# Taking both parts of x through one 512-column product in eight of twelve chunks, with VectorE adding the two sums

## The chip, the cores and the metric

The program runs on one core of a Trainium2 chip. Its engines, as the profile names them: PE (TensorE, matmul) with PEld (its weight loads), DVE (VectorE), ACT (ScalarE), POOL (GpSimd) and SP (SyncE, which issues the DMAs). The metric is the device time of one execution in microseconds; before the change three runs gave 743.53 (median), 743.38 and 745.63.

## The reference

Sliding-window attention with sink columns, followed by one two-layer block over all tokens:

```python
scores = scale * q @ k.T             # 4 batches, 8 heads, 768 positions, head_dim 64
keep = (pos_k < n_sink) | ((rel >= 0) & (rel < window))   # 4 and 128
a = softmax(where(keep, scores, -1e9))
x = (a @ v), heads side by side      # 3072 tokens x 512
h = x @ w_in                         # 512 -> 2048
sp = where(h > 20, h, log1p(exp(min(h, 20))))
out = (h * tanh(sp)) @ w_out         # 2048 -> 512
```

The weights are float64 and the rest is float32.

## The kernel before

The 3072 tokens are worked in 12 chunks of 256 tokens (T = 256, two row blocks of 128). For a chunk, four pairs of heads go through attention (`pair`): scores on PE (L386, L389), masking and row minimum on DVE (L397), exponential on ACT (L400), normalising (L404 to L411), transposes on PE (L421, L430), and the product with v (L439, L443) into a PSUM tile `att`. Its result is the chunk's x, transposed: for each pair of heads, 128 features by 256 tokens.

The matmuls run on float32r operands. To keep float32's precision, a value is split into an upper part, rounded to float32r, and a lower part, the rest; a product is then upper times upper, upper times lower and lower times upper. So x is stored as xh (a copy, L447) and xl (a subtraction on DVE, L448); a weight is prepared once as `wih`/`wil` or `woh`/`wol` in the first third of the span.

The two layers go in 8 steps per chunk (`step`), each over 256 of the 2048 hidden features, that is two blocks y of 128. The first layer fills one PSUM tile `hp` of 128 x 2 x 256, one half for each y. For a block there are four slices kt of 128 features of x and three products of 256 columns for each slice (L477, L478): weight upper by xh, weight upper by xl, weight lower by xh. A step therefore has 24 products of 256 columns, and all three sums land on the same 256 columns. There are two `hp` buffers. Then the activation runs on the whole 128 x 512 tile: Exp from PSUM (L486), a minimum on DVE (L487), Square, Ln and Exp on ACT (L488 to L490), and on DVE the product with `hp` (L491), which writes `n`. The second layer needs `gh`, a rounded copy of n (mostly ACT, L248), and `gl`, the difference (L261 on DVE or L259 on POOL, by the planner's choice). It adds 8 products of 512 columns with gh and 4 with gl to two accumulators `acc` (L506).

The order of all work is set before the program is built: `Plan.solve` takes tasks with a priority, a cost for each engine that may do them, and buffers, and always places next the task that can start earliest; `emit` then writes each engine's instructions in that order. A task is a group of instructions, such as six products of the first layer. A cost marked `shared` is not placed beside POOL work. Where the planner leaves PE without work for 250 ns or more, `emit` fills in products with zeros (L601). The first three chunks are interleaved, while weights are still being prepared; the other nine follow one by one, each chunk's attention running ahead during the chunk before it. The last chunk has no attention beside it.

Of the kernel before, what the change touches and what calls it, by code (L numbers as in the profile page):

```python
# [23 lines left out]
P = 128  # L24
# [33 lines left out]
def f32(ap):  # L58
    return ap.bitcast(F32)
# [6 lines left out]
def dve_t(n, fast=False):  # L66
    return ((n / 2 if fast else n) + 66) / 0.96
# [11 lines left out]
def pe_t(*ns):  # L79
    return sum(n / 2.4 + 13.3 for n in ns)  # L80
# [24 lines left out]
class Plan:  # L105
# [6 lines left out]
    def add(self, prio, ways, deps=(), bufs=(), new=()):  # L112
        deps = {id(d): d for d in list(deps) + [b.maker for b in bufs] if d is not None}
        t = Task(prio, ways, list(deps.values()), list(bufs) + list(new), list(new))
        for b in t.bufs:
            b.users += 1
        for b in new:
            b.maker = t
        self.tasks.append(t)
        return t  # L120
# [104 lines left out]
class Fast(Base):  # L225
# [128 lines left out]
    def pair(self, b, c3, pr, rank, x, x_done):  # L354
# [81 lines left out]
        def out():  # L436
# [4 lines left out]
            if not first:  # L441
# [1 line left out]
                    yield nc.tensor.matmul(o.t[:, i * P:(i + 1) * P], vr.t[:, i, :], sks.t, start=False, stop=i == TB - 1)  # L443
        cost = sum(c1 - c0 for _, c0, c1, _, _ in jobs) / .6 + 200 + (0 if first else T / .6 + 50)
        a = add(r + .05, {PE: (cost, out)}, last + ldv + vdeps, [pth, vt] + ([] if first else [vr, sks]), [o])
        (h, l), k, newx = x[pr // 2], pr % 2, pr % 2 == 0
        a = add(r + .15, self.copy_ways(T, lambda: h.t[:, k, :], lambda: o.t, True), [a], [o] + ([] if newx else [h]), [h] if newx else [])  # L447
        c = add(r + .17, self.sub_ways(T, lambda: l.t[:, k, :], lambda: o.t, lambda: f32(h.t[:, k, :]), (DVE,)), [a],  # L448
                [o, h] + ([] if newx else [l]), [l] if newx else [])
        x_done += [a, c]  # L450

    def jobs(self, first):
# [3 lines left out]

    def step(self, st, f2, rank, begins, ends, wdeps, last):

        nc, add = self.nc, self.plan.add
        if begins:
            st.acc, st.tail = [Buf("acc", [P, DM]) for _ in range(TB)], None
        x, acc = st.x, st.acc
        (wih, woh), (wil, wol) = ((w["wi"], w["wo"]) for w in (self.wh, self.wl))
        r = rank - (SH if last else 0)
        hp = Buf("att" if last and f2 % 2 else "hp", [P, 2, T])
        eager = last and f2 >= NF // 2 - QUICK
        g1 = []
        for y in range(2):  # L470
            f = 2 * f2 + y
            for kh in range(2):
                def first(f=f, y=y, kh=kh):
                    for kt in (2 * kh, 2 * kh + 1):
                        fs = slice(kt * P, (kt + 1) * P)
                        xh, xl = x[kh]
                        for n_, (w_, x_) in enumerate(((wih[f], xh), (wih[f], xl), (wil[f], xh))):  # L477
                            yield nc.tensor.matmul(hp.t[:, y, :], w_.t[:, fs], x_.t[:, kt % 2, :], start=kt == 0 and n_ == 0,  # L478
                                                   stop=kt == KT - 1 and n_ == 2)
                fr = y == 0 and kh == 0  # L480
                g1.append(add(r + .1 + .1 * y + .05 * kh, {PE: (pe_t(*[T] * 6), first)},
                              st.x_done[4 * kh:4 * kh + 4] + wdeps[f][0:2] + g1[-1:], list(x[kh]) + ([] if fr else [hp]), [hp] if fr else []))
        u, m = Buf("u", [P, 2, T]), Buf("n", [P, 2, T])
        gh, gl = Buf("gh", [P, 2, T], F32R), Buf("gl", [P, 2, T], F32R)
        N = 2 * T
        a = add(r + .5, {ACT: (act_t(N, True), lambda: nc.scalar.activation(u.t, hp.t, AF.Exp))}, g1, [hp], [u])  # L486
        a = add(r + .51, {DVE: shared((dve_t(N, True), lambda: nc.vector.tensor_scalar(u.t, u.t, E20, None, ALU.min)))}, [a], [u])  # L487
        a = add(r + .52, {ACT: (act_t(N, ptr=1), lambda: nc.scalar.activation(u.t, u.t, AF.Square, bias=self.one))}, [a], [u])  # L488
        a = add(r + .53, {ACT: (act_t(N, ptr=1), lambda: nc.scalar.activation(u.t, u.t, AF.Ln, bias=self.half, scale=0.5))}, [a], [u])  # L489
        a = add(r + .54, {ACT: (act_t(N), lambda: nc.scalar.activation(u.t, u.t, AF.Exp, scale=-1.0))}, [a], [u])  # L490
        e = add(r + .55, {DVE: (dve_t(N), lambda: nc.vector.scalar_tensor_tensor(m.t, u.t, 1.0, hp.t, ALU.subtract, ALU.mult))}, [a], [u, hp], [m])  # L491
        gg = add(r + .57, self.copy_ways(N, lambda: gh.t, lambda: m.t), [e], [m], [gh])
        gk = add(r + .58, self.sub_ways(N, lambda: gl.t, lambda: m.t, lambda: f32(gh.t)), [gg], [m, gh], [gl])
        if eager:
            del gk.ways[POOL]
            del gg.ways[ACT]
        r = rank
        for y, t, part in self.order(last and f2 == NF // 2 - 1):
            f = 2 * f2 + y
            new = begins and y == 0 and not part  # L500
            done = ends and y == 1 and part == 1

            def second(f=f, y=y, t=t, part=part, new=new, done=done):
                ts_ = slice(t * P, (t + 1) * P)
                for n_, (g_, w_) in enumerate(((gl, woh[f]),) if part else ((gh, woh[f]), (gh, wol[f]))):
                    yield nc.tensor.matmul(acc[t].t, g_.t[:, y, ts_], w_.t, start=new and n_ == 0, stop=done)  # L506
            st.tail = add(r + 1.45 + .2 * part + (.05 * y + .1 * t if last else .1 * y + .05 * t), {PE: (pe_t(*[512] * (2 - part)), second)},
                          [gk if part else gg, st.tail] + wdeps[f][2:4], [gl if part else gh] + ([] if new else [acc[t]]), [acc[t]] if new else [])
            if done:
                self.store(st, r, t, f2 == NF // 2 - 1)  # L510
# [34 lines left out]
    def run(self):  # L545
        self.plan = Plan(self.TAGS)
        self.setup()
        chunks = sorted(((b, c3) for b in range(B) for c3 in range(NCH)), key=lambda z: (z[1] > 0, z))
        self.wh, self.wl = ({"wi": [], "wo": []} for _ in range(2))
        wdeps = [self.weights(f, f * WA + WB) for f in range(NF)]  # L550
        states = []
        for n, (b, c3) in enumerate(chunks):
            st = SimpleNamespace(row=b * S + c3 * T, x_done=[], part={})
            st.x = [(Buf("w", [P, 2, T], F32R), Buf("w", [P, 2, T], F32R)) for _ in range(2)]
            for pr in range(NPAIR):
                self.pair(b, c3, pr, self.att_rank(n, pr), st.x, st.x_done)
            states.append(st)
        seq = self.sequence(len(chunks))
        for r, (n, f2) in enumerate(seq):
            begins, ends = r == 0 or seq[r - 1][0] != n, r + 1 == len(seq) or seq[r + 1][0] != n  # L560
            self.step(states[n], f2, r, begins, ends, wdeps, n == len(chunks) - 1)
        self.emit(self.plan.solve())

    def att_rank(self, n, pr):
# [307 lines left out]
```

## Time and profile before

| | before |
|---|---|
| median of three runs, us | 743.53 |
| profiled execution, us | 743.74 |
| its span, first to last instruction, us | 741.4 |
| PE busy, us (share of the span) | 728.5 (98%) |
| ACT busy, us | 585.4 (79%) |
| DVE busy, us | 474.0 (64%) |
| POOL busy, us | 136.4 (18%) |

The span is what one execution takes between its first and last instruction; some 2.3 us lie around it in the execution's own time. Matmuls are pipelined: a PE row's duration runs from the start to the modelled end of one product, and the next starts long before that. What a product takes from the stream is read from one start to the next.

### The profile page before, as it was taken

The page shows a single profiled execution, that of the slowest core. Times are in us where ns is not written, and L with a number is a line of the kernel's source. Part 1 is how long each engine was busy: PE and PEld are TensorE (multiplying, and loading weights), DVE is VectorE, ACT ScalarE, POOL GpSimd, SP SyncE. Part 2 cuts the span into 40 slices and gives each one's busy share as a digit, 9 for nine tenths or more (in the row PEclk, how much of TensorE's full clock was granted, in tenths as well). Part 3 has the DMA queues.
Part 4 walks back from the last instruction along what each step waited for, and adds up shares of the span by engine and source line. Part 5 has one row for each costly group of instructions (what it writes and reads, how often), then busy time and mean ns, then how long its engine had stood idle before and what let it go on. Part 6 is the DMA issues. An engine that isn't in the chain of part 4 may idle for free.

```text
span 741.4 us, 13855 instructions
## 1 busy us (share of the span) xinstructions
PE 728.5 (98%) x5042; PEld 638.5 (86%) x5042; DVE 474.0 (64%) x1258; ACT 585.4 (79%) x1284; POOL 136.4 (18%) x96
## 2 busy tenths in 40 slices
PE   8999999999999999999999999999999999999996
PEld 5767888888888888988898989889988999899995
DVE  6899899998676655557665556465555555543322
ACT  5999998887778778787778888887888788875753
POOL 0454431232001102200001211121122121110000
PEclk9999999999999999999999999999999999999999
DMA  6654333432342422422332333224313331100000
GB/s 190 180 161 131 121 130 114 137 114 57 107 131 60 103 73 79 106 73 72 92 94 72 90 77 91 72 59 99 100 43 79 105 75 43 49 18 1 29 1 34
DMA packets 48989, 64.17 MB, mean 87 GB/s; under 512 B 4880, under 2 KB 41744, under 8 KB 48912
## 3 DMA queue, kind: packets, MB, share of 16 engines
q1 hardware_dynamic: 48912, 63.20, 30.5%
q8 instruction: 42, 0.69, 0.4%
q14 instruction: 35, 0.29, 0.1%
HBM read 56.89 MB, written 6.29 MB: 85 GB/s over the span
## 4 chain that ended last, share of the span: by engine, by line
PE 82%; ACT 12%; DVE 3%; DMA 1%; issue 0%; ACTq 0%
PE acc L506 32%; PE hp L478 30%; PE att L439 5%; PE att L389 5%; PE att L421 4%; PE att L443 3%; ACT p L400 2%; ACT p L411 2%; PE att L478 2%; ACT w L280 2%; ACT w L248 1%; DMA raw<-w_out 1%; ACT pth L248 1%; ACT u L490 1%; ACT raw L290 1%; ACT u L489 1%
## 5 line engine op out<-in xcount | busy, mean ns | idle before, releaser
L478 PE MATMUL hp<-w,w 128*128 128x256 f32 x2208 | 299.7, 286 | 0.9 <-DVE n L491 0.8
L478 PEld LDWEIGHTS hp<-w,w 128*128 128x128 f32 x2208 | 277.6, 190 | 7.5 <-DVE n L491 1.9
L506 PE MATMUL acc<-w,gh 128*128 128x512 f32 x768 | 197.2, 394 | 0.0
L506 PEld LDWEIGHTS acc<-w,gh 128*128 128x128 f32 x768 | 136.8, 189 | 23.6 <-issue 0.5
L491 DVE SCALAR_TENSOR_TENSOR n<-u,hp 128x512 f32<-128x512 f32 x92 | 62.9, 685 | 72.8 <-ACT u L490 45.3
L506 PE MATMUL acc<-w,gl 128*128 128x512 f32 x384 | 107.6, 395 | 0.0
L400 ACT ACTIVATE p<-p,nm 128x288 f32<-128x288 f32 (+1 forms) x192 | 95.3, 497 | 12.4 <-DVE nm L397 12.3
L488 ACT ACTIVATE u<-u,bias 128x512 f32<-128x512 f32 x96 | 69.1, 721 | 35.5 <-DVE u L487 35.5
L487 DVE TENSOR_SCALAR u<-u 128x512 f32<-128x512 f32 x96 | 44.2, 461 | 74.7 <-ACT u L486 74.5
L397 DVE CUSTOM_DVE_ANT_0 p<-att,m 128x288 f32<-128x288 f32 (+1 forms) x192 | 75.7, 418 | 16.4 <-PE att L389 13.0
L506 PEld LDWEIGHTS acc<-w,gl 128*128 128x128 f32 x384 | 70.8, 188 | 14.4 <-DVE gl L261 0.3
L248 ACT ACTIVATE gh<-n 128x512 fp32r<-128x512 f32 x93 | 58.2, 626 | 27.9 <-DVE n L491 27.6
L411 ACT ACTIVATE p<-p,rc 128x288 f32<-128x288 f32 (+2 forms) x129 | 61.2, 502 | 23.0 <-DVE rc L405 22.5
L259 POOL TENSOR_TENSOR raw<-raw,raw 64x896 fp32r<-64x896 f32 x21 | 44.5, 2121 | 169.3 <-ACT raw L248 107.0
L486 ACT ACTIVATE u<-hp 128x512 f32<-128x512 f32 x92 | 54.3, 590 | 25.2 <-PE hp L478 24.7
L489 ACT ACTIVATE u<-u,bias 128x512 f32<-128x512 f32 x96 | 69.0, 720 | 2.1
L261 DVE TENSOR_TENSOR gl<-n,gh 128x512 fp32r<-128x512 f32 x74 | 52.5, 710 | 26.5 <-ACT gh L248 13.5
L490 ACT ACTIVATE u<-u 128x512 f32<-128x512 f32 x96 | 60.0, 626 | 1.7
L421 PE MATMUL att<-ident,p 128*128 128x128 f32 x352 | 55.6, 275 | 2.9 <-DVE rc L404 1.3
L259 POOL TENSOR_TENSOR gl<-n,gh 128x512 fp32r<-128x512 f32 x22 | 29.2, 1329 | 152.7 <-ACT gh L248 114.8
L439 PE MATMUL att<-pth,vt 128*64 128x128 f32 (+1 forms) x504 | 47.9, 322 | 0.4 <-ACT pth L248 0.2
L421 PEld LDWEIGHTS att<-ident,p 128*128 128x128 f32 x352 | 40.9, 140 | 8.4 <-ACT p L411 1.9
(83 smaller groups left out, 817.0 us busy)
## 6 DMA issues: line engine op xcount, KB each, us to landing
raw<-k_p SPq DMA_DIRECT2D x64, 224.0 KB, 3.6
raw<-w_in SPq DMA_DIRECT2D x16, 512.0 KB, 3.7
raw<-w_out SPq DMA_DIRECT2D x16, 512.0 KB, 4.1
w<-q_p SPq DMA_DIRECT2D x64, 128.0 KB, 3.5
y<-u SPq DMA_DIRECT2D x24, 256.0 KB, 2.2
vt<-v_b SPq DMA_DIRECT2D x32, 192.0 KB, 2.5
vsr<-v_s SPq DMA_DIRECT2D x32, 128.0 KB, 2.3
ks<-k_p SPq DMA_DIRECT2D x15, 144.0 KB, 2.2
```

The costliest lines, as they stand in the source:

```text
L248: ways[ACT] = act_t(n, psum), lambda: nc.scalar.activation(dst(), src(), AF.Copy, scale=scale or 1.0)
L259: ways[POOL] = pool_t(n), lambda: nc.gpsimd.tensor_tensor(dst(), a(), b(), ALU.subtract)
L397: a = add(r + .03 + .01 * e, {DVE: (dve_t(n) + 8, lambda st=st, pv=pv, nm=nm, e=e, mask=mask, n=n: nc.vector.tensor_tensor_reduce(out=pv() ...
L400: a = add(r + .05 + .01 * e, {ACT: (act_t(n, ptr=2), lambda pv=pv, nm=nm, sm=sm, e=e: nc.scalar.activation(pv(), pv(), AF.Exp, bias=nm.t[: ...
L411: ACT: (act_t(n, ptr=1), lambda row=row, rc=rc, e=e: nc.scalar.activation(row(), row(), AF.Copy, scale=rc.t[:, e:e + 1]), 0, PEN_N),
L421: yield nc.tensor.transpose(pt.t[:, e, x * P:(x + 1) * P], p2.t[:, i, e, cols[x]:cols[x] + P], self.ident)
L439: yield nc.tensor.matmul(o.t[e * D:(e + 1) * D, o0:o1], vt.t[:, e, j, :], pth.t[:, e, c0:c1], start=n_ == 0, stop=first and n_ == len(jobs ...
L478: yield nc.tensor.matmul(hp.t[:, y, :], w_.t[:, fs], x_.t[:, kt % 2, :], start=kt == 0 and n_ == 0, stop=kt == KT - 1 and n_ == 2)
L488: a = add(r + .52, {ACT: (act_t(N, ptr=1), lambda: nc.scalar.activation(u.t, u.t, AF.Square, bias=self.one))}, [a], [u])
L489: a = add(r + .53, {ACT: (act_t(N, ptr=1), lambda: nc.scalar.activation(u.t, u.t, AF.Ln, bias=self.half, scale=0.5))}, [a], [u])
L490: a = add(r + .54, {ACT: (act_t(N), lambda: nc.scalar.activation(u.t, u.t, AF.Exp, scale=-1.0))}, [a], [u])
L506: yield nc.tensor.matmul(acc[t].t, g_.t[:, y, ts_], w_.t, start=new and n_ == 0, stop=done)
```

## The change

In chunks 3 to 10 (`wide`), xh and xl of a slice lie side by side in one tile of 128 x 2 x 256. One product of 512 columns takes both with the weight's upper part, and writes two separate sums: upper by xh in the first half of the PSUM tile, upper by xl in the second. The product of the weight's lower part with xh, 256 columns as before, is added to the first half. A tile `hp` now holds one block y, so a step uses two of them; a `tensor_reduce` on DVE adds the two halves into `n`, one instruction for each y, as soon as that block is done. The activation and the last multiplication then read `n` in SBUF in place of `hp` in PSUM, and the multiplication (now `shared` for the planner) writes over `n`. The other four chunks compute as before, with x kept in the new layout.

```diff
-        (h, l), k, newx = x[pr // 2], pr % 2, pr % 2 == 0
-        a = add(r + .15, self.copy_ways(T, lambda: h.t[:, k, :], lambda: o.t, True), ...)
-        c = add(r + .17, self.sub_ways(T, lambda: l.t[:, k, :], lambda: o.t, lambda: f32(h.t[:, k, :]), (DVE,)), [a], ...)
+        h = x[pr]
+        a = add(r + .15, self.copy_ways(T, lambda: h.t[:, 0, :], lambda: o.t, True), [a], [o], [h])
+        c = add(r + .17, self.sub_ways(T, lambda: h.t[:, 1, :], lambda: o.t, lambda: f32(h.t[:, 0, :]), (DVE,)), [a], [o, h])
...
-        hp = Buf("att" if last and f2 % 2 else "hp", [P, 2, T])
+        if not wide:
+            hp = Buf("att" if last and f2 % 2 else "hp", [P, 2, T])
         for y in range(2):
             f = 2 * f2 + y
+            if wide:
+                hp = Buf("hp", [P, 2, T])
             for kh in range(2):
...
+                        if wide:
+                            yield nc.tensor.matmul(hp.t, wih[f].t[:, fs], xt, start=kt == 0, stop=False)
+                            yield nc.tensor.matmul(hp.t[:, 0, :], wil[f].t[:, fs], xt[:, 0, :], start=False, stop=kt == KT - 1)
+                            continue
...
+            if wide:
+                hs.append(add(r + .3 + .1 * y, {DVE: (dve_t(2 * T), lambda y=y, hp=hp: nc.vector.tensor_reduce(
+                    m.t[:, y, :], hp.t.rearrange("p z t -> p t z"), mybir.AxisListType.X, ALU.add))}, ...))
+        h = m if wide else hp
-        a = add(r + .5, {ACT: (act_t(N, True), lambda: nc.scalar.activation(u.t, hp.t, AF.Exp))}, g1, [hp], [u])
+        a = add(r + .5, {ACT: (act_t(N, not wide), lambda: nc.scalar.activation(u.t, h.t, AF.Exp))}, hs or g1, [h], [u])
...
-        e = add(r + .55, {DVE: (dve_t(N), lambda: nc.vector.scalar_tensor_tensor(m.t, u.t, 1.0, hp.t, ALU.subtract, ALU.mult))}, [a], [u, hp], [m])
+        way = dve_t(N), lambda: nc.vector.scalar_tensor_tensor(m.t, u.t, 1.0, h.t, ALU.subtract, ALU.mult)
+        e = add(r + .55, {DVE: shared(way) if wide else way}, [a], [u, h], [] if wide else [m])
...
-            st.x = [(Buf("w", [P, 2, T], F32R), Buf("w", [P, 2, T], F32R)) for _ in range(2)]
+            st.x = [Buf("w", [P, 2, T], F32R) for _ in range(KT)]
```

What this does to the order is shown at three places. First PE, in the middle of the kernel before: one block y of the first layer, after the scores of a pair (the `w` on the left of the comma is a part of x, the other a part of a weight).

```order
L389 MATMUL att_2176_1_5021<-raw_2032_0_4702,w_1963_0_4540 128x288
L478 MATMUL hp_2177_0_5026<-w_1659_0_3830,w_898_0_2137 128x256
L478 MATMUL hp_2177_0_5026<-w_1662_0_3836,w_898_0_2137 128x256
L478 MATMUL hp_2177_0_5026<-w_1659_0_3830,w_903_0_2143 128x256
L478 MATMUL hp_2177_0_5026<-w_1659_0_3830,w_898_0_2137 128x256
L478 MATMUL hp_2177_0_5026<-w_1662_0_3836,w_898_0_2137 128x256
L478 MATMUL hp_2177_0_5026<-w_1659_0_3830,w_903_0_2143 128x256
```

The same place of a wide chunk in the changed kernel, a whole block y, up to the next one:

```order
L443 MATMUL att_1748_0_3930<-sks_1730_0_3900,vsr_1616_0_3660 128x128 x2
L483 MATMUL hp_1755_0_3948<-w_1359_0_3127,w_563_0_1436 128x512
L484 MATMUL hp_1755_0_3948<-w_1359_0_3127,w_573_0_1453 128x256
L483 MATMUL hp_1755_0_3948<-w_1441_0_3297,w_563_0_1436 128x512
L484 MATMUL hp_1755_0_3948<-w_1441_0_3297,w_573_0_1453 128x256
L483 MATMUL hp_1755_0_3948<-w_1522_0_3466,w_563_0_1436 128x512
L484 MATMUL hp_1755_0_3948<-w_1522_0_3466,w_573_0_1453 128x256
L483 MATMUL hp_1755_0_3948<-w_1615_0_3658,w_563_0_1436 128x512
L484 MATMUL hp_1755_0_3948<-w_1615_0_3658,w_573_0_1453 128x256
L421 MATMUL att_1765_0_3971<-ident_100,p2_1712_0_3860 128x128 x4
L483 MATMUL hp_1768_0_3978<-w_1359_0_3127,w_621_0_1553 128x512
```

Three products of a slice have become two, and each block y has an `hp` tile of its own.

Second DVE, in the kernel before, from one step's minimum (L487) to that step's multiplication (L491) and beyond:

```order
L487 TENSOR_SCALAR u_2193_0_5075<-u_2193_0_5075 128x512
L251 COPY pth_2206_0_5101<-att_2184_0_5049 128x2x256
L261 TENSOR_TENSOR w_2123_0_4910<-att_2197_0_5082,w_2120_0_4904 128x256
L491 SCALAR_TENSOR_TENSOR n_2218_0_5118<-u_2193_0_5075,hp_2177_0_5026 128x512
L397 ISA p2_2223_0_5137,nm_2223_1_5138<-att_2220_0_5122,m2_114 128x288
L397 ISA nm_2223_1_5138 128x1
L261 TENSOR_TENSOR gl_2224_0_5141<-n_2218_0_5118,gh_2221_0_5128 128x512
```

DVE in a wide chunk of the changed kernel, from one step's multiplication (now L501, with `n` on both sides) to the next step's minimum (now L497):

```order
L501 SCALAR_TENSOR_TENSOR n_1774_0_3993<-u_1780_0_4004,n_1774_0_3993 128x512
L493 TENSOR_REDUCE n_1802_0_4048<-hp_1792_0_4024 128x256
L404 TENSOR_SCALAR rc_1805_0_4057<-sm_1793_2_4031 128x2
L405 RECIPROCAL rc_1805_0_4057<-rc_1805_0_4057 128x2
L261 TENSOR_TENSOR gl_1809_0_4063<-n_1774_0_3993,gh_1804_0_4055 128x512
L410 TENSOR_SCALAR p2_1793_0_4029<-p2_1793_0_4029,rc_1805_0_4057 128x288
L493 TENSOR_REDUCE n_1802_0_4048<-hp_1803_0_4050 128x256
L497 TENSOR_SCALAR u_1818_0_4080<-u_1818_0_4080 128x512
```

The two reductions (L493) stand between the steps, the second directly ahead of the minimum whose input it feeds through ACT's Exp.

Third PE at the first wide step of the changed kernel. The order of PE's products before this place is the same in both kernels up to some 150 products ahead of it.

```order
L389 MATMUL att_1288_1_2973<-raw_1139_0_2651,w_1214_0_2812 128x288
L421 MATMUL att_1292_0_2983<-ident_100,p2_1222_0_2834 128x128 x4
L612 LDWEIGHTS zero_75
L612 MATMUL acc_1260_0_2920<-zero_75 128x224
L612 LDWEIGHTS zero_75
L612 MATMUL acc_1260_0_2920<-zero_75 128x224
L517 MATMUL acc_1255_0_2906<-w_1070_0_2501,gh_1291_0_2981 128x512
```

Here two products with zeros are filled in that the kernel before does not have. They are the only ones that were added, and none follows them; there are 164 in the kernel before and 166 now. Over the whole program 1024 products of 256 columns (2208 to 1184) became 512 of 512 columns. On DVE 128 reductions are new; the planner also moved work: the subtraction of the keys' parts (64 x 896) goes 30 times to DVE (11 before) and 2 times to POOL (21), the gl subtraction 59 times to DVE (74) and 37 to POOL (22), and the copy of x's upper part out of PSUM 15 times to DVE (38) and 33 to ACT (10).

## Rows read from the trace of the kernel before

**Rows 1.** The page: span, busy shares, PE and its clock in 40 slices.

```profile
span 741.4 us, 13855 instructions
PE 728.5 (98%) x5042; PEld 638.5 (86%) x5042; DVE 474.0 (64%) x1258; ACT 585.4 (79%) x1284; POOL 136.4 (18%) x96
PE   8999999999999999999999999999999999999996
PEclk9999999999999999999999999999999999999999
```

**Rows 2.** Busy time by stage (windows of 50 us), from 200 to 650 us.

```profile
core 0: us, PE busy (x) PEld busy (x) DVE busy (x) ACT busy (x) POOL busy (x), PEclk, DMA share, GB/s
200.00:250.00 50.00, 50.00 (x345) 44.25 (x345) 31.14 (x84) 39.16 (x87) 4.69 (x3) 1.00 0.36 99
...
600.00:650.00 50.00, 50.00 (x359) 44.96 (x358) 28.46 (x76) 41.31 (x90) 10.27 (x6) 1.00 0.20 56
sum 450.00, PE 450.00 PEld 403.01 DVE 266.12 ACT 362.14 POOL 75.75; mean PE 50.00 PEld 44.78 DVE 29.57 ACT 40.24 POOL 8.42
```

**Rows 3.** Chain that ended last, in order of time: start, length (us), what.

```profile
193.19 2.95 PE acc L506 x12
...
347.35 2.87 PE hp L478 x24
...
538.67 2.75 PE acc L506 x12
```

**Rows 4.** Two steps in the middle, all engines: start, length (us), engine, line, operation.

```profile
468.27 0.61 ACT L248 ACTIVATE gh<-n 128x512 fp32r<-128x512 f32 x1
...
472.06 1.70 PEld L506 LDWEIGHTS acc<-w,gh 128*128 128x128 f32 x8
...
472.38 0.60 ACT L486 ACTIVATE u<-hp 128x512 f32<-128x512 f32 x1
...
476.37 0.63 ACT L248 ACTIVATE gh<-n 128x512 fp32r<-128x512 f32 x1 [0.76 <-DVE n L491]
...
478.74 1.69 PEld L506 LDWEIGHTS acc<-w,gh 128*128 128x128 f32 x8
...
480.69 1.07 PE L506 MATMUL acc<-w,gl 128*128 128x512 f32 x4
...
481.60 0.56 PE L389 MATMUL att<-raw,w 128*128 128x288 f32 x3
```

**Rows 5.** PE alone over a step and the start of the next two.

```profile
404.28 2.00 PE L506 MATMUL acc<-w,gh 128*128 128x512 f32 x8
...
412.53 2.00 PE L506 MATMUL acc<-w,gh 128*128 128x512 f32 x8
...
419.20 1.09 PE L506 MATMUL acc<-w,gh 128*128 128x512 f32 x4
```

**Rows 6.** Groups by line: instructions near the reduction, the activation and the moved work.

```profile
L491 DVE SCALAR_TENSOR_TENSOR n<-u,hp 128x512 f32<-128x512 f32 x92 | 62.9, 685 | 72.8 <-ACT u L490 45.3 <-PE att L389 24.3 <-PE hp L478 2.2
L261 DVE TENSOR_TENSOR gl<-n,gh 128x512 fp32r<-128x512 f32 x74 | 52.5, 710 | 26.5 <-ACT gh L248 13.5 <-PE acc L506 12.7
L251 DVE COPY pth<-att 128x512 f32<-128x512 f32 (+1 forms) x28 | 18.5, 661 | 10.2 <-PE att L421 9.4
L251 DVE CAST w<-att 128x256 fp32r<-128x256 f32 x38 | 16.1, 423 | 6.3 <-PE att L443 5.1 <-PE att L439 0.5
L261 DVE TENSOR_TENSOR raw<-raw,raw 64x896 fp32r<-64x896 f32 x11 | 12.0, 1089 | 1.2 <-ACT raw L248 0.9
L486 ACT ACTIVATE u<-hp 128x512 f32<-128x512 f32 x92 | 54.3, 590 | 25.2 <-PE hp L478 24.7
L490 ACT ACTIVATE u<-u 128x512 f32<-128x512 f32 x96 | 60.0, 626 | 1.7
L259 POOL TENSOR_TENSOR gl<-n,gh 128x512 fp32r<-128x512 f32 x22 | 29.2, 1329 | 152.7 <-ACT gh L248 114.8 <-PE hp L478 18.9 <-PE att L421 13.3
L601 PE MATMUL acc<-zero 128*128 128x224 bf16 x164 | 21.0, 272 | 0.0
```

More of the change, by code (lines that the diff above doesn't have):

```diff
@@ L445, in pair @@
         a = add(r + .05, {PE: (cost, out)}, last + ldv + vdeps, [pth, vt] + ([] if first else [vr, sks]), [o])
-        (h, l), k, newx = x[pr // 2], pr % 2, pr % 2 == 0
-        a = add(r + .15, self.copy_ways(T, lambda: h.t[:, k, :], lambda: o.t, True), [a], [o] + ([] if newx else [h]), [h] if newx else [])
-        c = add(r + .17, self.sub_ways(T, lambda: l.t[:, k, :], lambda: o.t, lambda: f32(h.t[:, k, :]), (DVE,)), [a],
-                [o, h] + ([] if newx else [l]), [l] if newx else [])
+        h = x[pr]
+        a = add(r + .15, self.copy_ways(T, lambda: h.t[:, 0, :], lambda: o.t, True), [a], [o], [h])
+        c = add(r + .17, self.sub_ways(T, lambda: h.t[:, 1, :], lambda: o.t, lambda: f32(h.t[:, 0, :]), (DVE,)), [a], [o, h])
         x_done += [a, c]
@@ L455, in jobs, with step @@
         return (1, P, 2 * T - P, 0, T), (0, 0, P, 0, P), (2, 2 * T - P, 2 * T, P, T)
-    def step(self, st, f2, rank, begins, ends, wdeps, last):
+    def step(self, st, f2, rank, begins, ends, wdeps, last, wide):
         nc, add = self.nc, self.plan.add
@@ L466, in step @@
         r = rank - (SH if last else 0)
-        hp = Buf("att" if last and f2 % 2 else "hp", [P, 2, T])
         eager = last and f2 >= NF // 2 - QUICK
[L469 to L482, printed above, removed]
         u, m = Buf("u", [P, 2, T]), Buf("n", [P, 2, T])
@@ L485, in step, with first @@
         N = 2 * T
-        a = add(r + .5, {ACT: (act_t(N, True), lambda: nc.scalar.activation(u.t, hp.t, AF.Exp))}, g1, [hp], [u])
+        g1, hs = [], []
+        if not wide:
+            hp = Buf("att" if last and f2 % 2 else "hp", [P, 2, T])
+        for y in range(2):
+            f = 2 * f2 + y
+            if wide:
+                hp = Buf("hp", [P, 2, T])
+            for kh in range(2):
+                def first(f=f, y=y, kh=kh, hp=hp):
+                    for kt in (2 * kh, 2 * kh + 1):
+                        fs, xt = slice(kt * P, (kt + 1) * P), x[kt].t
+                        if wide:
+                            yield nc.tensor.matmul(hp.t, wih[f].t[:, fs], xt, start=kt == 0, stop=False)
+                            yield nc.tensor.matmul(hp.t[:, 0, :], wil[f].t[:, fs], xt[:, 0, :], start=False, stop=kt == KT - 1)
+                            continue
+                        for n_, (w_, z) in enumerate(((wih[f], 0), (wih[f], 1), (wil[f], 0))):
+                            yield nc.tensor.matmul(hp.t[:, y, :], w_.t[:, fs], xt[:, z, :], start=kt == 0 and n_ == 0,
+                                                   stop=kt == KT - 1 and n_ == 2)
+                fr = kh == 0 and (wide or y == 0)
+                g1.append(add(r + .1 + .1 * y + .05 * kh, {PE: (pe_t(*([2 * T, T] * 2 if wide else [T] * 6)), first)},
+                              st.x_done[4 * kh:4 * kh + 4] + wdeps[f][0:2] + g1[-1:], x[2 * kh:2 * kh + 2] + ([] if fr else [hp]), [hp] if fr else []))
+            if wide:
+                hs.append(add(r + .3 + .1 * y, {DVE: (dve_t(2 * T), lambda y=y, hp=hp: nc.vector.tensor_reduce(
+                    m.t[:, y, :], hp.t.rearrange("p z t -> p t z"), mybir.AxisListType.X, ALU.add))}, [g1[-1]], [hp, m] if y else [hp], [] if y else [m]))
+        h = m if wide else hp
+        a = add(r + .5, {ACT: (act_t(N, not wide), lambda: nc.scalar.activation(u.t, h.t, AF.Exp))}, hs or g1, [h], [u])
         a = add(r + .51, {DVE: shared((dve_t(N, True), lambda: nc.vector.tensor_scalar(u.t, u.t, E20, None, ALU.min)))}, [a], [u])
@@ L560, in run @@
             begins, ends = r == 0 or seq[r - 1][0] != n, r + 1 == len(seq) or seq[r + 1][0] != n
-            self.step(states[n], f2, r, begins, ends, wdeps, n == len(chunks) - 1)
+            self.step(states[n], f2, r, begins, ends, wdeps, n == len(chunks) - 1, GROUP <= n < len(chunks) - 1)
         self.emit(self.plan.solve())
```

## The prediction

> **What bounds the kernel now.** I read the page first. PE is busy 98% of the span, at the full clock in all 40 slices but for the two ends [rows 1]. A busy share alone could still hide waits, so the second view is the stages: from 200 to 650 us PE is busy 450.00 of 450 us, while ACT has 362 and DVE 266, that is 80% and 59% [rows 2]. The reader is to see that in this stretch no other engine is ever waited for, and that only what PE streams can be won there. The third view is the chain, for the price of that stream: it strings together runs of like products from start to start. 24 products of 256 columns take 2.87 us, 119.6 ns each; 12 of 512 columns take 2.75 us, 229.2 ns each [rows 3]. Twice the columns cost less than twice the time: a product has a part that does not grow with its columns. The fourth view, all engines in two steps, says how far the work behind PE is from being late [rows 4].
>
> **The sum on PE.** Per slice kt the change replaces two products of 256 columns by one of 512, and leaves the third. 8 chunks x 8 steps x 2 blocks x 4 slices are 512 replacements. Two products of 256 take 239.2 ns. For one of 512 the rows give three prices. The chain's ordinary run has 229.2 ns: 10.0 ns saved, 5.1 us in all. The four gl products from 480.69 to the next task at 481.60 have 227.5 ns [rows 4]: 11.7 ns saved, 6.0 us. The worst run of the chain has 2.95 us for 12, 245.8 ns [rows 3]: 6.6 ns lost, +3.4 us in all. The first two are nearly all of the stream and lie close together; the worst stands at 193 us, at the end of the crowded early stage, and I keep it for the range. I take the middle of the first two, 5.6 us. Weight loads fall by 512 as well, but PEld is busy 403 of 450 us beside a full PE [rows 2] and ends nothing, so I cost them at nothing; that the fixed part of a product may be a piece of its load is already in the measured prices.
>
> Against this stand two filled-in products of zeros at the first wide step, the only new ones. All 164 before took 21.0 us [rows 6], 0.128 us each: 0.3 us. They also say that the planner sees one pause there and no other of its filling size later.
>
> **What is added on DVE.** 128 reductions, each reading 128 x 512 from PSUM and writing 128 x 256. No row shows a reduction. From below: if it cost by what it writes, the 128 x 256 copy out of PSUM has 423 ns. By what it reads: the 128 x 512 copy out of PSUM has 661 ns, the multiplication with a PSUM operand 685. From above, two passes: 1370 ns, twice the latter [rows 6]. I take 685: it reads 512 elements and has an operand in PSUM, as that row does. Two steps last from 404.28 to 419.20, so one has 7.46 us [rows 5], of which DVE is busy 59%, 4.40 us. Two reductions make it 5.77 of some 7.37 us, 78%. The multiplication with both inputs in SBUF goes from 685 to the 710 ns of the gl subtraction, ACT's Exp from 590 to the 626 of L490 [rows 6]. The planner's moves about cancel on DVE: 19 more key subtractions of 1089 ns add 20.7 us, 15 fewer gl subtractions of 710 ns and 23 fewer copies of 423 ns take 20.4 us away. So neither DVE nor ACT comes to bound a step by its load; PE's 100% is the cover under which all of this costs nothing.
>
> **What it does to the latency.** The added reduction is a wait: Exp of a step now starts only after the second reduction, and PE's second layer waits for gh. What stands before it in DVE's order is listed with the change: the previous gl subtraction and a normalisation. In the rows of before, gh is ready at 468.27 + 0.61 = 468.88 and its first weight load starts at 472.06, 3.18 us later; in the next step gh is ready at 477.00 and loaded at 478.74, 1.74 us later [rows 4]. The steps alternate, the shorter one being that without the product with v. The chain grows by the second reduction 0.685, the Exp 0.036 and the multiplication 0.025, 0.75 us, and the time given to it shrinks by 8 x 10.9 ns, 0.09. So about 0.9 us are left in the tight steps, 2.3 in the others. The `hp` buffers cannot be what is late next: a buffer was held through Exp, four more operations and the multiplication, and is now free after its reduction, so two for a step last longer than two for two steps did. The two `n` buffers are held longer instead, from the first reduction to the gl subtraction, about the time that an `hp` was held before.
>
> **Total.** 743.74 (the profiled execution, 0.2 us over the median of the runs) - 5.6 + 0.3 = 738.4 us. The first 150 us, the last chunk and the output are unchanged by the order.
>
> **Rivals.**
> *Queueing gives it back.* The tight steps have 0.9 us left. A key subtraction of 1089 ns that DVE has begun when the second reduction could start, or a gl subtraction of 0.71 and a normalisation of 0.38 before it as in the listed order, is 0.15 to 0.2 us more than that. In all 32 tight steps this makes 4.8 to 6.4 us, and the time 743.2 to 744.8. For it: DVE's order is fixed and it is 78% full. Against it: PE may stand at other work then, since the order was made with the reductions in it and shows no filling product, and at 80% load ACT kept every such wait from PE. The multiplication may be held up as well: POOL is busy 75.75 of 450 us [rows 2], mostly in reads of SBUF, and a gl subtraction there takes 1329 ns [rows 6]; meeting one half-way in 17% of the steps would be 0.11 us a step on average, inside the 0.9. The Trainium skill bears on this point (SBUF — State Buffer, Who interferes with whom): a VectorE instruction with two SBUF inputs contends with a GpSimd one that reads SBUF, where one with a PSUM operand does not. By that rule the change makes L491's successor open to such waits, by the trace they fit in the slack; it moves this rival's chance from 0.08 to 0.10.
>
> *Only columns count.* In the alternation of 512 and 256 columns the fixed part could stay, because each product has a new weight to load and the stream has as many columns as before. Then nothing is won, and the time is 743.74 + 0.3 = 744.0. Rows 3 speak against it: both sorts of product there had a load each, and 229.2 is less than 239.2. The Trainium skill has a rule near this (TensorE: Matmul & The Clock Gate, Back-to-back issue gap): warm products follow each other by N/2.4 ns and a fixed 2.5 ns. By that rule the 512 merged products would save 1.3 us and the time would be 742.7; the trace disagrees, with 119.6 ns for 256 columns where the rule has 109. Chance 0.05.
>
> *The reduction is dear.* At 1370 ns, two of them take 2.74 us a step, DVE is at 4.40 + 2.74 + 0.03 of 7.37 us, 97%, and the slack of a tight step falls to 1.74 - 1.37 - 0.06 - 0.09 = 0.22 us. Any instruction ahead of it, some 0.7 us, then makes PE wait about 0.5 us; in 32 steps 16 us, and the time is about 754. It decides from a reduction of about 1.0 us on, where one such instruction ahead eats what is left. For it: it reads its input at a stride of 256 elements, two at a time, which no row shows. Against it: nothing in the rows has a 512-element DVE operation on float32 beyond 0.7 us save those that convert. The Trainium skill calls this operation the slowest of VectorE and advises against it on a hot path (VectorE: DVE Perf Modes, Rules for kernel authors); no run here shows it yet. Chance 0.09.
>
> **How the numbers follow.** Forecast 0.76, queueing 0.10, only columns 0.05, dear reduction 0.09. What this kernel's measurement can tell from no change is about 0.3%, 2.2 us. The forecast's own range is 737 to 741 (the two prices of the product, and a microsecond or two of small waits). Queueing and only columns end within 0.3% and are 0.15, of which I give 0.02 to slower, for queueing that goes on past its price; 0.02 of the forecast falls within 0.3% by its upper tail. So faster 0.74, same 0.15, slower 0.11. The range of 8 in 10 goes from 736 to 744, up to the two rivals in the middle, and leaves out the dear reduction and the worst price of a product.
>
> **What would show it.** In the profile after: PE still busy all of each 50 us window in the wide chunks; a slice's two products some 347 ns apart from the next slice's (227.5 to 229.2 + 119.6); `n<-hp` TENSOR_REDUCE x128 near 0.68 us; DVE near 78% in those windows; no waits of PEld for gh or for an `hp` buffer. Wrong would be: a reduction above 1 us, PE waiting for `n` or gh in every second step, or 512-column products at 235 ns and more.

## The result and the profile after

The changed kernel takes 740.0 us (median of 7 runs, 738.4 to 741.59); the kernel before, on the same chips, 744.35 us (7 runs, 743.38 to 745.63). The ratio is 0.9947, with a 95% interval of 0.9935 to 0.9959: 3.9 us faster, where 5.3 were forecast. The profiled execution took 739.4 us, 4.3 less than that of before.

The page of the changed kernel: span and busy shares.

```profile
span 737.6 us, 13009 instructions
PE 723.5 (98%) x4532; PEld 610.7 (83%) x4532; DVE 536.8 (73%) x1365; ACT 591.3 (80%) x1300; POOL 126.0 (17%) x101
```

The sum of busy time by stage, from 200 to 650 us, as in [rows 2]:

```profile
sum 450.00, PE 449.78 PEld 380.95 DVE 324.18 ACT 368.10 POOL 64.89; mean PE 49.98 PEld 42.33 DVE 36.02 ACT 40.90 POOL 7.21
```

PE is as full as before, 449.78 of 450 us; DVE went from 59% to 72%, ACT from 80% to 82%. So the bound is the same, and what was won inside this stretch was won in PE's stream. The chain of the changed kernel at three places (start, length, what):

```profile
150.89 2.75 PE acc L517 x12
...
565.76 2.75 PE acc L517 x12
...
580.56 2.75 PE acc L517 x12
...
687.16 2.87 PE att L487 x24
```

and the rows of the kernel before that answer to them:

```profile
151.61 2.75 PE acc L506 x12
...
568.50 2.75 PE acc L506 x12
...
583.41 2.75 PE acc L506 x12
...
690.91 2.87 PE att L478 x24
```

Two steps take 580.56 - 565.76 = 14.80 us where they took 14.91: 0.11 us for 16 slices, 7 ns a slice, 3.6 us for all 512. The last two rows are the same place in the last chunk, 3.75 us earlier. Of these, 0.72 us are there already at 151 us, where both kernels have the same order: a difference between two executions, not the change. The wide chunks themselves gave 3.0 us net.

The two profiled executions differ by 4.3 us, their spans by only 3.8. Some 0.5 us of the gain lies outside the span: in every execution of the kernel before whose span is on record, 2.1 to 2.5 us lie around it, in those of the changed kernel and of its variants 1.75 to 1.9. No run here shows why, and nothing in the argument of the change gives it.

### The profile page after: what moved, and what is told of

Read it like the earlier page. It is cut to its first block, busy times and chain, and to the rows that moved or that the text cites. A ratio compares the mean times of both kernels' runs of the same rounds, so it can differ in the third digit from the quotient of the medians.

```text
span 737.6 us, 13009 instructions
## 1 busy us (share of the span) xinstructions
PE 723.5 (98%) x4532; PEld 610.7 (83%) x4532; DVE 536.8 (73%) x1365; ACT 591.3 (80%) x1300; POOL 126.0 (17%) x101
## 4 chain that ended last, share of the span: by engine, by line
PE 76%; ACT 14%; DVE 5%; DMA 2%; issue 1%; ACTq 0%; DVEq 0%
PE acc L517 30%; PE hp L483 15%; PE hp L484 8%; PE hp L487 5%; PE att L439 4%; PE att L389 4%; PE att L421 4%; PE att L443 3%; ACT p L400 2%; ACT p L411 2%; PE att L487 2%; ACT w L248 2%; ACT w L280 1%; DMA raw<-w_out 1%; ACT u L498 1%; ACT gh L248 1%
## 5 line engine op out<-in xcount | busy, mean ns | idle before, releaser
L483 PE MATMUL hp<-w,w 128*128 128x512 f32 x512 | 191.7, 409 | 0.0
L484 PE MATMUL hp<-w,w 128*128 128x256 f32 x512 | 143.2, 280 | 0.0
L493 DVE TENSOR_REDUCE n<-hp 128x256 f32<-128x512 f32 x128 | 88.1, 689 | 19.7 <-PE hp L484 18.4
L259 POOL TENSOR_TENSOR gl<-n,gh 128x512 fp32r<-128x512 f32 x37 | 47.9, 1294 | 307.6 <-ACT gh L248 223.2
L498 ACT ACTIVATE u<-u,bias 128x512 f32<-128x512 f32 x96 | 69.2, 722 | 31.1 <-DVE u L497 31.0
L487 PE MATMUL hp<-w,w 128*128 128x256 f32 x672 | 91.3, 286 | 0.9 <-DVE n L501 0.8
L487 PEld LDWEIGHTS hp<-w,w 128*128 128x128 f32 x672 | 85.2, 191 | 6.3 <-DVE n L501 1.9
L497 DVE TENSOR_SCALAR u<-u 128x512 f32<-128x512 f32 x96 | 43.5, 453 | 50.3 <-ACT u L496 50.2
L496 ACT ACTIVATE u<-n 128x512 f32<-128x512 f32 x64 | 40.4, 631 | 47.9 <-DVE n L493 47.8
L248 ACT ACTIVATE gh<-n 128x512 fp32r<-128x512 f32 x93 | 58.4, 627 | 20.7 <-DVE n L501 19.1
```

The source lines that it names most:

```text
L248: ways[ACT] = act_t(n, psum), lambda: nc.scalar.activation(dst(), src(), AF.Copy, scale=scale or 1.0)
L483: yield nc.tensor.matmul(hp.t, wih[f].t[:, fs], xt, start=kt == 0, stop=False)
L484: yield nc.tensor.matmul(hp.t[:, 0, :], wil[f].t[:, fs], xt[:, 0, :], start=False, stop=kt == KT - 1)
L487: yield nc.tensor.matmul(hp.t[:, y, :], w_.t[:, fs], xt[:, z, :], start=kt == 0 and n_ == 0, stop=kt == KT - 1 and n_ == 2)
L493: hs.append(add(r + .3 + .1 * y, {DVE: (dve_t(2 * T), lambda y=y, hp=hp: nc.vector.tensor_reduce(m.t[:, y, :], hp.t.rearrange("p z t -> p ...
```

## The experiments

**Only the merged product undone.** Everything else of the change stays: layout, reductions, moved work.

```diff
-yield nc.tensor.matmul(hp.t, wih[f].t[:, fs], xt, start=kt == 0, stop=False)
+yield nc.tensor.matmul(hp.t[:, 0, :], wih[f].t[:, fs], xt[:, 0, :], start=kt == 0, stop=False)
+yield nc.tensor.matmul(hp.t[:, 1, :], wih[f].t[:, fs], xt[:, 1, :], start=False, stop=False)
```

> The changed kernel with only the merged product undone: in the wide chunks a slice again has three products of 256 columns (upper by xh and lower by xh into the first half of hp, upper by xl into the second). Layout, reductions, moved work and the order on every other engine stay as in the change. Theory 1, all of the gain is the fixed part of the 512 merged products and the reductions cost PE next to nothing: the time goes back to that of the kernel before or just over it, ratio to before 1.000 to 1.003 (744 to 746 us), two steps take 14.9 us again where the change has 14.80, and PE shows no waits of size. Rival A, part of the gain comes from elsewhere (hp buffers free earlier, the moved subtractions, the early stage): the ratio stays at 0.995 to 0.998 (740.5 to 743). Rival B, the reductions cost PE hidden time that the merged product pays for: the ratio is 1.004 or more (over 747).

Measured: 744.23 us, ratio to before 1.0001 (0.9990 to 1.0012). Its chain has the same step to step as before, 14.92 us for two:

```profile
561.92 2.75 PE acc L518 x12
...
576.84 2.75 PE acc L518 x12
```

The gain is the merged product's: 4.2 us lie between this run and the change. All the rest together, the 128 reductions, the second `hp` tile and the moved work, changes the time by nothing that can be measured; by the medians the span is 0.3 us longer than before (742.4 against 742.1), and the 0.5 us outside it are won in this run too. Both rivals fall.

**What a product costs in a sequence.** A program of products alone, one stretch after another.

> Not the reference's computation: a program of matmuls alone, on a slice of q, that prices runs of products with nothing beside them and writes a piece of a result to every row. Stretches: three products of 256 columns a slice (as before), 512 and 256 in turn (as in the change), 512 512 256 256, 512 alone, 24 of 256 followed by 12 of 512, and 512 and 256 in turn beside reductions on DVE and Exp on ACT that read other places. Theory 1, the price of a 512-column product depends on its neighbours on PE: in turn with 256 it takes 232 to 236 ns, alone 227, and after a run of 256 some 233 at first and 227 later; a slice takes 358 ns as three and 350 in turn, and the stretch beside DVE and ACT is the same as without. Rival, the other engines' reads of PSUM or SBUF make it dearer: without them 227 + 120 = 347 a slice, beside them 350 or more.

Measured, from the start of one stretch to the start of the next, 24 slices each (L104 begins three products of 256 columns, L109 those with 512):

```profile
63.58 0.28 PE L104 MATMUL three<-x,wh 128*128 128x256 f32 x1
...
72.21 0.40 PE L109 MATMUL wide<-x,wh 128*128 128x512 f32 x1
...
80.69 0.40 PE L109 MATMUL pairs<-x,wh 128*128 128x512 f32 x1
...
89.05 0.40 PE L109 MATMUL big<-x,wh 128*128 128x512 f32 x1
```

Three of 256 take (72.21 - 63.58) / 24 = 359.6 ns a slice, 512 and 256 in turn 353.3, and 512 512 256 256 348.3. The stretch of 512 alone is one row of the chain:

```profile
33.12 10.91 PE big L109 x48
```

that is 227.3 ns each. So 227 is the price in a long run of its own kind; 227.3 + 119.9 would be 347 a slice, and in turn a slice costs 6 ns more. The mean from one start to the next tells which of the two is dearer: in turn, a product of 512 takes 236.5 ns and one of 256 takes 117.2. Twelve products of 512 behind 24 of 256 take 2.75 us, 229.2 each, as in the kernel's own rows. It is not the other engines: the reductions and Exps meant for the last stretch came earlier, beside the first stretch of products in turn (16.12 to 24.60 us; reductions over most of it, the Exps until 19.6), and that has 8.48 us as the one from 72.21 to 80.69, which has no reduction or Exp beside it.

```profile
16.12 0.40 PE L109 MATMUL wide<-x,wh 128*128 128x512 f32 x1
...
24.60 0.40 PE L109 MATMUL pairs<-x,wh 128*128 128x512 f32 x1
...
16.88 6.48 DVE L148 TENSOR_REDUCE m<-other 128x256 f32<-128x512 f32 x9
```

Theory 1 holds in kind, at 353 a slice where 350 was expected.

**512, 512, 256, 256 in the kernel.**

```diff
-for kt in (2 * kh, 2 * kh + 1):      # 512 then 256 for each slice
+for lo in range(2):                  # both 512, then both 256
+    for kt in (2 * kh, 2 * kh + 1):
```

> The changed kernel with another order inside a task of two slices: 512, 512, 256, 256 columns in place of 512, 256, 512, 256. Same products, columns and weights. In the change a slice takes about 350 ns, a 512-column product 232 to 240 in place of the 227.5 that the gl products have. Theory 1, each change from 256 to 512 columns costs some 6 ns: with half as many changes a slice takes 347 ns, 512 x 3 ns = 1.5 us less than the change (738.5 us against 740.0, ratio to before 0.9925). Rival, the price of a product depends on the two products' streams and loads alone, or on its place after a longer run: the same as the change within 0.5 us, ratio 0.994 to 0.996.

Measured: 740.47 us, ratio to before 0.9945 (0.9928 to 0.9962), the same as the change; two steps take 14.80 us here too:

```profile
566.72 2.75 PE acc L522 x12
...
581.52 2.75 PE acc L522 x12
```

The theory, 347 ns a slice, would have made them 14.75, so it falls for the kernel; the rows say so more sharply than the time does. The 5 ns a slice that the long stretches showed are not there in its short runs of 4 to 8 products between transposes and scores. For the merge, prices from a long stretch said which way and not how much; for the order they did not even say which way.

**The reduction done twice.**

```diff
+for _ in range(2):
     nc.vector.tensor_reduce(m.t[:, y, :], hp.t.rearrange("p z t -> p t z"), ...)
```

> The changed kernel with every reduction done twice, one after the other, into the same place; the second changes nothing in the result, and the order is that of the change. This makes the reduction as dear as the prediction's third rival had it (1.37 us). In the change gh is ready 0.8 us (median of 69 steps from 200 to 660 us) before its first weight load. The second instruction takes DVE 0.6 us more per block. Theory 1, the slack is what hides the reductions: the median slack goes to 0.2 us or less, PE waits for gh in a third to a half of the steps, and the time rises by 5 to 15 us over the change (745 to 755, ratio to before 1.001 to 1.015), DVE 88 to 93% busy in the windows from 200 to 650 us. Rival, DVE's free quarter hides this too: within 1 us of the change (739 to 741), no waits on PE.

Measured: 805.92 us, ratio 1.0825 (1.0803 to 1.0847): 66 us over the change. The kind of wait was as expected; its amount was expected more than four times too small, and DVE is 79% busy from 220 to 650 us where 88 to 93 were expected. Waits of the run with both doubled, 200 to 700 us (total, times, longest):

```profile
PEld acc L519 <- ACT gh L248: 60.2, 51, 2.3
PE acc L519 <- ACT gh L248: 44.0, 45, 1.9
```

The timeline gives what was added. Two reductions one after the other:

```profile
567.74 1.41 DVE L495 TENSOR_REDUCE n<-hp 128x256 f32<-128x512 f32 x2
```

A single one takes 0.69 us, so the second adds 0.72, not the 0.6 that the expectations reckon with: the second starts 0.718 us (median) after the first, while another operation starts 0.61 after a reduction. A step had 1.44 us more on DVE and lost 1.03, so only 0.4 us of it found room, half the slack of 0.8 us at gh. Which part of the added work counts, the next two runs ask.

**One of the two reductions doubled**: that of y = 1, or that of y = 0.

```diff
+for _ in range(2 if y == 1 else 1):      # the other run: y == 0
     nc.vector.tensor_reduce(...)
```

> The changed kernel with only the second reduction of each step (that of y = 1, whose end Exp waits for) done twice; order as in the change. It adds 0.6 us of DVE per step, half of what the run with both doubled added (which took 805.9 us, 66 us or 1.03 us a step over the change, with PE waiting 44 us for gh). Theory 1, latency: the chain second reduction - Exp - minimum - Square - Ln - Exp - multiplication - gh is what PE comes to wait for, and only what lies on it counts. The slack of 0.8 us (median) hides most of 0.6: +2 to +10 us over the change (742 to 750). Rival, load: DVE's fixed order is a queue in which any added work is late for all behind it, so half the added work costs half: about +33 us (773).

> As the run before it, but the first reduction of each step (y = 0) is done twice and the second once: the same 0.6 us of DVE per step, at a place from which Exp is still one block of the first layer (1.4 us) and one more reduction away. Theory 1, latency: less on the chain than the doubled second reduction: 0 to +3 us over the change (740 to 743), and less than that run. Rival, load: the same as that run, about +33 us.

Measured: 760.27 us with the second doubled (ratio 1.0228, 1.0213 to 1.0243) and 769.6 us with the first (1.0357, 1.0342 to 1.0372): 20 and 30 us over the change. The latency theory falls: the reduction further from Exp costs more. The load theory is nearer, with 33 expected for both, but DVE is not full. Busy time from 220 to 650 us, first the change, then the run with the first reduction doubled:

```profile
220.00:650.00 430.00, 429.78 (x2591) 363.89 (x2590) 309.46 (x777) 351.94 (x768) 62.29 (x47) 1.00 0.30 79
```

```profile
220.00:650.00 430.00, 413.44 (x2439) 341.48 (x2437) 328.87 (x785) 331.19 (x723) 57.11 (x43) 1.00 0.29 76
```

All engines have idle time there: PE 96%, DVE 76%, ACT 77%. What binds is in the chain of that run, over two steps (start, length, what; the first row of each step is its multiplication):

```profile
567.83 0.69 DVE n L503
...
569.85 0.91 DVE rc L404
...
570.95 0.59 DVE pth L251
...
571.73 0.61 DVE n L495
...
572.37 0.64 ACT u L498
...
574.88 0.94 ACT raw L248
...
575.84 1.10 DVE raw L261
...
576.96 0.69 DVE n L503
...
584.12 0.69 DVE n L503
```

PE is not in it. From one multiplication (L503) through the next step's reductions (L495), a normalisation (L404) and a copy of the attention (L251), Exp (L498), a copy and a subtraction of keys (L248, L261) to the next multiplication, and on through the next step in much the same way, without the keys: 584.12 - 567.83 = 16.29 us for two steps. DVE's and ACT's orders are fixed, and the attention's instructions stand in them between those of the two layers. A late reduction delays the attention's instructions behind it, these come late before the next step's, and the loop closes without PE. That is what the chain of this run shows. In the run with the second doubled the chain from 560 to 592 us still passes through PE once. Why the first reduction costs more than the second is not shown; in one of the two steps of its chain the normalisation L404 behind it takes 0.91 us, in the other run's chain 0.09.

The order in all these runs is the one that was planned with a single reduction. What an order planned for the longer work would cost was not run, so the losses are those of added work in a given order.

**Half of it, in every second step.**

```diff
+for _ in range(2 if y and f2 % 2 == 1 else 1):      # the other run: == 0
```

> The changed kernel with the second reduction done twice in every odd step only: 0.6 us more DVE per two steps, 32 times. Doubled in every step it cost 20 us (0.63 us per two steps for 1.2 us of added work). In the changed kernel gh is ready 0.76 us before its load in one kind of step and 0.8 to 1.1 us in the other. Theory 1, loop: DVE's and ACT's fixed order closes a loop over two steps, which has some 0.6 us to spare against PE's 14.80 us; 0.6 us added anywhere in the loop just fits: 0 to +3 us over the change (740 to 743), the same for odd and even steps. Theory 2, local slack: only the step's own 0.76 to 1.1 us at gh counts, and 0.6 us always fits: no change, 739.5 to 740.5, in both runs. Rival, load: half of the 20 us, +10 us (750) in both runs.

> The same with the even steps in place of the odd ones. Loop: 740 to 743, within 1.5 us of the odd run. Local slack: 739.5 to 740.5. Load: 750.

Measured: 745.63 us (ratio 1.0022, 1.0009 to 1.0035) and 746.28 us (1.0032, 1.0022 to 1.0042): 5.6 and 6.3 us over the change. All three figures fail: both times lie above the loop's range and the local slack's, and below the load's 750. The two kinds of step are alike. With 0.72 us for a second reduction, per two steps (32 of them) 0.72 us added cost 0.2; 1.44 us cost 0.63 and 0.93; 2.87 us cost 2.06. On average 0.5 to 0.8 us in 14.8 found room, some 3.5 to 5.5%.

The loss is not even. With the odd steps doubled, two steps still take 14.80 us in long stretches (from 436 to 456 us the chain is PE alone), and 15.0 to 15.2 in others. So at this dose a loop does not bind everywhere. And local slack falls only as the expectation put it, with 0.76 us and more at every step: in the change's trace gh is ready between 0.05 and 2.7 us before its load (median 0.76), in 21 of the 64 wide steps less than 0.72. Adding up by how much 0.72 us exceeds each step's own slack gives, as an estimate, 6.9 us for all steps and half of that for every second one. Measured were 20 (second reduction) and 30 (first), and 5.6 and 6.3. So a good part of the small loss can be plain local slack; the larger ones are lateness that is passed on from step to step.

**The change in the first three chunks too.**

```diff
-GROUP <= n < len(chunks) - 1
+n < len(chunks) - 1
```

> The change made in the first three chunks too (wide from chunk 0 on, not the last), where weights are still being prepared and DVE is busy 92 to 95% from 50 to 150 us while PE has 23 us of waits in the first 150 us. The planner fills in 100 more products of zeros than in the change. 24 more steps: 192 merged products win at most 1.4 us, 48 reductions add 29 us of DVE at 0.6 us each. Theory, in this stage DVE is the bound and every reduction is paid: +15 to +30 us over the change (755 to 770, ratio to before 1.015 to 1.035). Rival, PE's waits in that stage are for DMA and ACT and the reductions fit: within 2 us of the change.

Measured: 754.04 us, ratio 1.0132 (1.0115 to 1.0149), 14 us over the change. Just under the lower end, but on the theory's side. Busy time of that run from 100 to 150 us (DVE is the third busy number), then of the kernel before:

```profile
100.00:150.00 50.00, 49.88 (x275) 39.77 (x275) 49.24 (x108) 45.57 (x103) 13.86 (x10) 1.00 0.37 115
```

```profile
100.00:150.00 50.00, 48.90 (x319) 43.18 (x317) 47.63 (x97) 43.02 (x84) 12.25 (x9) 1.00 0.38 115
```

DVE goes from 95 to 98%, and PE's busy time there is partly products of zeros, 266 in this program where the kernel before has 164. From 160 to 170 us PE is busy only 7.55 us, and the granted clock of the next 10 us is 0.85, where it is 1.00 in the change: by that some 1.5 us of the 14, as an estimate, are the clock's. The same edit wins where PE is the bound and loses where DVE is.

**The change in six steps of the last chunk too.**

```diff
-hp = Buf("hp", [P, 2, T])
+hp = Buf("att" if last and y else "hp", [P, 2, T])
...
-GROUP <= n < len(chunks) - 1
+GROUP <= n and (n < len(chunks) - 1 or f2 < NF // 2 - QUICK)
```

> The change extended to the first six of the last chunk's eight steps, where DVE is 20 to 50% busy; the last two steps, whose latency ends the program, stay as they are. 48 more merged products (6 steps x 8 slices) at 7 ns each are 0.35 us, in long runs without attention between them perhaps 10 ns, 0.5 us: 739.5 to 739.7 us where the change has 740.0, ratio to before 0.994. Rival, the longer chain is in the way where two chunks' work no longer overlaps: 0.5 to 2 us slower than the change.

Measured: 740.02 us, ratio 0.9958 (0.9943 to 0.9972). No difference from the change can be seen; half a microsecond could not be, so this decides nothing.

## Why the prediction was right, and where it was off

**The bound** held: PE, and the merged product, which the first experiment shows to be the gain inside the span. The forecast was 738.4 us, the profiled execution took 739.4 and the median is 740.0. That it came so close is in part luck: 0.5 us were won outside the span, which nothing in the sum stands for.

**The size of the product** is the term that was off. I priced the merged product at 227.5 to 229.2 ns, from runs of products of 512 columns among their own kind, and saved 10.9 ns a slice, 5.6 us. In turn with 256 it costs more; a slice saved 7 ns, 3.6 us. PE in the changed kernel, one block and half of the next:

```profile
577.05 0.39 PE L483 MATMUL hp<-w,w 128*128 128x512 f32 x1
...
579.15 0.27 PE L421 MATMUL att<-ident,p 128*128 128x128 f32 x1
```

Six slices in 579.15 - 577.05 = 2.10 us, 350 ns each, where 347 to 349 were expected. From 300 to 650 us a product of 512 between two of 256 takes 233.9 ns on average to the next start, and one of 256 between two of 512 takes 116.3; the first is just below the 235 at which the prediction would have called itself wrong. The same kind of place in the kernel before:

```profile
475.45 1.58 PE L478 MATMUL hp<-w,w 128*128 128x256 f32 x12
...
476.88 0.60 PE L421 MATMUL att<-ident,p 128*128 128x128 f32 x4
```

Four slices in 1.43 us are 357.5 each, not the 358.8 of the long runs in [rows 3]. The saving is some 7 ns and not 10.9. About two thirds of the miss lie in the new slice (350 where the sum has 347.9) and one third in the old one (357.5 where it has 358.8).

**The reduction and what goes with it** were priced well: 689 ns for 685, the multiplication 691 for 710, Exp 631 (L496) for 626.

```profile
L493 DVE TENSOR_REDUCE n<-hp 128x256 f32<-128x512 f32 x128 | 88.1, 689 | 19.7 <-PE hp L484 18.4
L501 DVE SCALAR_TENSOR_TENSOR n<-u,n 128x512 f32<-128x512 f32 x64 | 44.2, 691 | 18.0 <-ACT u L500 17.3
```

DVE's share is 72% and not 78%. In a small part that is because I added whole durations, while the next operation starts 0.61 us after a reduction of 0.69: the 118 reductions of the window are 81 us long, but take some 77. For the most part the other work on DVE became some 20 us less in these 450 us. The moves did not cancel there, and L404 alone went from 19.5 to 11.4 us.

**The slack at gh** was half right. The changed kernel's two kinds of step:

```profile
564.12 0.61 ACT L248 ACTIVATE gh<-n 128x512 fp32r<-128x512 f32 x1
...
565.48 1.69 PEld L517 LDWEIGHTS acc<-w,gh 128*128 128x128 f32 x8
...
572.22 0.63 ACT L248 ACTIVATE gh<-n 128x512 fp32r<-128x512 f32 x1
...
573.66 0.54 PEld L517 LDWEIGHTS acc<-w,gh 128*128 128x128 f32 x3
```

0.75 us in the tight one (0.9 expected), and 0.81 in the other, where I expected 2.3 and [rows 4] had 3.18. Nearly all of the missing 1.5 us are not the reductions'. Here is that other step from its Exp to its multiplication, with the subtraction of the keys that now stands between them:

```profile
566.52 0.63 ACT L496 ACTIVATE u<-n 128x512 f32<-128x512 f32 x1 [0.41 <-DVE n L493]
...
570.38 1.09 DVE L261 TENSOR_TENSOR raw<-raw,raw 64x896 fp32r<-64x896 f32 x1 [0.72 <-ACT raw L248]
...
571.50 0.69 DVE L501 SCALAR_TENSOR_TENSOR n<-u,n 128x512 f32<-128x512 f32 x1
```

and the step of the kernel before that has the 3.18 us:

```profile
464.14 0.59 ACT L486 ACTIVATE u<-hp 128x512 f32<-128x512 f32 x1
...
467.40 0.69 DVE L491 SCALAR_TENSOR_TENSOR n<-u,hp 128x512 f32<-128x512 f32 x1 [2.21 <-PE att L389]
```

From Exp to the multiplication it is 4.98 us where it was 3.26. In the order before, POOL did this subtraction after the multiplication (2.12 us from 468.44). The planner moved it to DVE, ahead of the multiplication, and with it the copy of the keys on ACT. The prediction counted the moved subtractions as load alone, which about cancelled, and gave their place in the chain no price. The same two instructions stand in the chain of the run with the first reduction doubled; whether that run would lose less with the keys left on POOL is open. A second step of the prediction that failed is taking the slack of one consumer for the room of the whole, as the doubled reductions show.

**The rivals.** Queueing did not give the gain back. Waits of PE's loads for gh from 200 to 690 us (total, times, longest):

```profile
PEld acc L517 <- ACT gh L248: 0.7, 2, 0.5
```

Only columns: false, though the trace came a third of the way towards it. The Trainium skill's figure for the gap (TensorE: Matmul & The Clock Gate, Back-to-back issue gap), a fixed 2.5 ns, would by the prediction's estimate have made 742.7 us. The prediction did not say that the section gives this for a product by itself, and for a stream of loads and products another figure, 131 ns for 512 columns. The trace agrees with neither: at a granted clock of 1.00 it has 119.9 and 227.3 ns in uniform runs, some 13 to 14 ns over their columns at 2.4 GHz, and 740.0 us. The dear reduction did not come; the doubled one shows that its mechanism was real and its price wrong, 806 us in place of about 754, since I charged only the tight steps and only what exceeded their slack. Of the Trainium skill's warning about the operation (VectorE: DVE Perf Modes, Rules for kernel authors), the trace shows that this reduction costs what a multiplication of the same input does.

The multiplication with two SBUF inputs was not held up by GpSimd in the change, but that is no test: none of the 64 ran beside a POOL instruction, since the planner keeps them apart (`shared`). Where they do meet, the runs show the wait. In the run with the first three chunks changed, 7 of 88 ran beside POOL work and took 998 ns on average, the longest 1.77 us; the 81 others took 689. That longest one and the POOL work beside it:

```profile
103.56 1.77 DVE L501 SCALAR_TENSOR_TENSOR n<-u,n 128x512 f32<-128x512 f32 x1
102.22 2.56 POOL L259 TENSOR_TENSOR w<-w,w 128x512 fp32r<-128x512 f32 x2 [3.69 <-ACT w L248]
```

With one operand in PSUM there is no such wait. Of the 92 in the kernel before, 14 ran beside POOL work and took 674 to 689 ns, for example

```profile
75.55 0.68 DVE L491 SCALAR_TENSOR_TENSOR n<-u,hp 128x512 f32<-128x512 f32 x1
75.30 1.29 POOL L298 TENSOR_TENSOR w<-w,w 128x512 f32<-128x512 f32 x1
```

So this part of the queueing rival has a real mechanism, at a price of up to 1.1 us for a meeting; in the change the planner's order kept it away.

## What to carry to other kernels

Where PE is full, merging two products under one weight is worth work on an engine that has room: it won about 7 ns for each pair here, where the prices of uniform runs (2 x 119.9 - 227.3) promise 12. Price the product from a row in the sequence in which it will stand, not from a run of its own kind. Work that a planner moves to another engine has a place as well as a load: look at what it now stands in front of. Room on an engine with a fixed order is not its idle share, nor the median slack at one place where another engine takes over: double the added instruction and see. Here DVE had a quarter of its time free and 0.8 us at the hand-over, and 0.72 us more per two steps already cost, in the order as planned.

## What the runs showed that I had not expected

Products of 512 columns cost 227 ns in a long run of their own, but in turn with products of 256 a pair of the two cost 353.3 ns and not 347, and as much with DVE busy beside it; with 512 512 256 256 it was 348.3. In the kernel it was 350 in either order. Why is open; no run here separates the weight load from the rest.

Lateness does not stay where it arises. With DVE idle 28% of the time, 1.44 us of added work per two steps cost up to 0.93 us, and 2.87 us cost 2.06.

A VectorE multiplication with two SBUF inputs took up to 1.77 us beside GpSimd work, and 0.69 with one input in PSUM or with nothing beside it.
